# Query and key tiles on 128 partitions, the low parts of the first weights through TensorE and ScalarE, and a new table of places

## The chip, the cores and the metric

The kernel runs on one core of one Trainium2 chip. The metric is device time in microseconds (us), the median of several executions. TensorE multiplies into PSUM, VectorE, ScalarE and GpSimd do the element work, and all loads of the first stage are issued by SyncE (SP in the rows).

## What is computed

A stabilised linear attention with gates, then a dense layer with a softmax and a layer norm, then a mixture of eight experts with one expert for each token:

```
m = max(f + m, i);  C = exp(f + m_old - m) C + exp(i - m) v k^T;  n likewise with k
y = sigmoid(o) * (C q) / max(|n q|, 1)               # B=4, H=8, S=768, D=40
x = y as 3072 x 320
h = x @ w_in;  u = h * softmax(h);  z = layernorm(u) * g  @ w_out     # 320 -> 1024 -> 320
expert = argmax(norm(z) @ norm(emb)^T / tau);  out = gate * relu(z @ w1[e]) @ w2[e]
```

All weights come as 64-bit words and the result has to be exact to fp32, so that each weight is decoded on VectorE from integer words and split into a high and a low fp32r part, and each product is made of two or three fp32r matmuls.

## The kernel before

3072 tokens are cut into 24 blocks of 128 (`g` = 0 to 23; six blocks for each of the four batches). Every piece of work is a *step* with a key, an engine and a function; a step is added to a plan with `add(key, engine, ...)`, and the table `AT` gives each key a number. `Plan.order` sorts the steps by it, and the program is emitted in that order: each engine's queue is in order, so that an instruction whose input is late holds everything behind it on its engine.

The stages are these.

- **The start** (lines 321 to 570). SP issues the gates `gt`, the constants `cs` (which hold the identity), the embedding `em`, six loads of `w_in` (`rawwi`, 512 KB each), four of `w_out` (`rawwo`, 640 KB each) and the first blocks' `qk` (queries and keys, transposed) and `nat` (keys, values, output gates). There are four raw buffers, and each is given back by its decode. Up to eight loads are under way: SP waits for the load eight places ahead before it issues the next. VectorE decodes each raw tile in three instructions (`decode`, L408 to L410) and runs the scans over the gates (L352 to L366). TensorE transposes `w_out` (step `wtr`, L497), sums it (`cm`, L492) and multiplies it with the embedding (`ep`, L510, eight columns wide). 24 products of the identity with itself (`fill`, L577) stand between.
- `w_in` is split per piece j: ScalarE rounds it to fp32r (`whi`, `in_hi`, L428), and VectorE subtracts that from the decoded weight (`wlo`, `in_lo`, L434 and L436).
- **The blocks**. For each g: the scores S (L603), their mask `Pt` (VectorE, L608), the values `num` (L617), the carried state (L622), the new state `stc` (L627), the gate and the row X, its transpose `tpx` (L651), then the first dense layer `mm1` (L666 to L671; it needs all of `wlo`), softmax and norm, transposes `tpu`, the second layer `mm2` (L724 to L726) and the routing.
- **The experts**. When blocks are routed, weights `wr` and rows `xgr` of each expert are loaded, transposed (`txr`, L1093), multiplied (`m1` L1115, `m2` L1154) and scattered to the result (L1168).

Of the kernel before, what the change touches and what calls it, by code (L numbers as in the profile page):

```python
# [10 lines left out]
F32R = mybir.dt.float32r  # L11
# [52 lines left out]
    "ld_c": "138",  # L64
    "ld_e": "65",
# [3 lines left out]
    "mk": "328",  # L69
    "gmax0": "62",  # L70
    "glog0": "688",
    "gsum0": "701",
    "isub0": "682",
    "iadd0": "707",
    "iexp0": "718",
    "fexp0": "712",
    "itr0": "728",
    "icp0": "735",
    "ftr0": "726",
    "fcp0": "769",  # L80
    "gmax1": "68",
    "glog1": "88",
    "gsum1": "713",
    "isub1": "162",
    "iadd1": "736",
    "iexp1": "754",
    "fexp1": "738",
    "itr1": "801",
    "icp1": "817",
    "ftr1": "787",  # L90
    "fcp1": "805",
    "bad": "733",
    "badp": "749",
    "badc": "757",
    "f_in": "39 74 26 204 333 381",
    "dec_in": "177 215 291 374 453 590",
    "whi": "230 256 332 416 494 638",
    "wlo": "253 363 351 439 534 671",
    "emb1": "169",
    "emb2": "184",  # L100
    "emb3": "337",
    "emb4": "408",
    "emb5": "428",
    "f_out": "9 349 417 495",
    "dec_out": "118 490 546 627",
    "cm": "296 307 557 588 623 629 685 704",
    "wtr": "166 335 538 545 634 599 690 697",
    "wtc": "190 350 549 561 650 628 702 724",
    "ep": "443 462 568 613 665 675 716 739",
    "cmb": "785",  # L110
    "eg": "753",
    "esum": "763",
    "ecm": "812",
    "ecmb": "822",
    "ecen": "844",
    "eohi": "853",
    "eolo": "1039",
    "cen": "873 955 803 850",
    "ohi": "907 980 827 892",
    "olo": "957 998 856 911",  # L120
    "fill": "262 279 318 345 353 362 371 379 418 427 435 454",
    "load_q": "18 231 276 116 183 908 1071 1254 1441 1733 1953 2262 2413 2654 2893 3195 3379 3566 3814 4123 4363 4588 4773 5045",
    "load_n": "91 298 158 252 849 960 1122 1307 1501 1795 2015 2326 2502 2689 2980 3230 3442 3628 3874 4177 4413 4625 4835 5093",
    "vprep": "742 841 826 887 942 1036 1199 1385 1583 1871 2142 2403 2579 2766 3088 3315 3518 3704 4000 4253 4489 4701 4913 5170",
    "tprep": "220 433 287 380 925 1057 1204 1384 1578 1886 2092 2402 2649 2770 3057 3332 3527 3706 3951 4268 4509 4735 4912 5182",
    "smat": "117 388 816",
    "pv": "770 874",
    "smm": "761 866",
    "pmul": "264 277 412 426 976 989 1118 1132 1303 1330 1497 1510 1790 1805 2011 2025 2260 2274 2428 2441 2685 2699 2916 2930 3226 3240 3377 3391 3564 3577 3870 3883 4121 4186 4362 4421 4620 4647 4771 4785 5043 5103 5291 5304 5448 5462 5627 5641",
    "state": "773 880 1070 1253 1440 1952 2261 2412 2658 2892 3378 3565 3813 4122 4365 4772 5044 5239 5437 5580",  # L130
    "den": "791 912 1086 1270 1439 1732 1979 2287 2466 2653 2944 3194 3405 3591 3837 4135 4375 4587 4798 5056 5241 5436 5604 5882",
    "og": "823 924 1098 1282 1476 1769 1991 2299 2478 2665 2956 3206 3417 3603 3849 4147 4387 4600 4810 5068 5253 5476 5654 5894",
    "xdup": "848 959 1147 1312 1513 1794 2039 2325 2512 2707 3006 3251 3441 3635 3898 4176 4412 4624 4850 5102 5302 5500 5711 5939",
    "xtr": "857 993 1183 1333 1601 1812 2118 2408 2650 2786 3017 3274 3458 3653 3975 4256 4451 4713 4860 5123 5329 5576 5794 5953",
    "xh": "870 1004 1194 1344 1643 1830 2129 2424 2697 2803 3040 3286 3474 3664 3987 4278 4462 4725 4879 5134 5345 5592 5806 5966",
    "xl": "901 1028 1212 1358 1660 1843 2143 2455 2712 2822 3054 3303 3491 3677 3999 4298 4480 4755 4898 5159 5370 5616 5849 5985",
    "mm1": "916 956 1101 1148 1296 1340 1483 1608 1818 1855 2041 2077 2268 2304 2472 2508 2749 2792 2981 3024 3201 3238 3373 3413 3616 3714 3903 3939 4129 4174 4370 4415 4595 4631 4806 4867 5050 5087 5247 5283 5444 5481 5675 5712 5878 5917 6061 6098",
    "negmax": "1003 1187 1380 1686 1896 2119 2345 2549 2833 3065 3278 3453 3754 4010 4215 4455 4672 4945 5127 5332 5521 5753 5961 6141",
    "expo": "1032 1216 1409 1715 1924 2151 2373 2577 2862 3093 3307 3483 3783 4039 4243 4484 4700 4973 5156 5360 5550 5781 6000 6186",
    "umul": "1061 1245 1451 1744 1954 2186 2404 2606 2891 3134 3336 3512 3812 4068 4272 4513 4729 5002 5216 5389 5579 5810 6029 6215",  # L140
    "lnstat": "1091 1274 1480 1773 1983 2243 2432 2636 2920 3196 3365 3542 3841 4097 4302 4542 4759 5046 5245 5419 5608 5840 6058 6252",
    "lnvar": "1119 1317 1529 1803 2012 2273 2461 2670 2950 3224 3394 3576 3871 4145 4338 4571 4788 5074 5276 5449 5637 5876 6090 6282",
    "lnrs": "1150 1348 1561 1834 2043 2333 2492 2701 2982 3285 3426 3607 3902 4187 4369 4603 4819 5106 5306 5480 5668 5928 6134 6313",
    "utr": "1090 1138 1288 1474 1644 1592 1892 1804 1987 2032 2256 2463 2454 2581 2740 2731 2972 2963 3190 3317 3449 3608 3599 3696 3884 3893 4117 4165 4358 4406 4583 4668 4851 4843 5039 5235 5320 5432 5667 5658 5786 5837 6052 6043 6174 6220 6303 6349",
    "uh": "1105 1151 1300 1518 1657 1631 1904 1858 2000 2045 2300 2488 2500 2602 2791 2779 2989 2977 3205 3341 3462 3623 3612 3715 3904 3960 4133 4181 4377 4419 4599 4681 4868 4855 5055 5251 5333 5477 5716 5699 5816 5903 6065 6133 6211 6268 6330 6387",
    "ul": "1146 1167 1316 1533 1673 1647 1920 1874 2038 2061 2321 2504 2518 2632 2809 2795 3007 2993 3253 3361 3478 3641 3627 3731 3919 3976 4172 4199 4408 4435 4633 4696 4885 4871 5089 5318 5356 5496 5732 5715 5836 5935 6097 6166 6240 6285 6359 6407",
    "mm2": "1249 1435 1519 1556 1728 1767 1948 1996 2125 2161 2418 2545 2659 2695 2888 2927 3060 3101 3281 3465 3560 3660 3809 3848 3986 4022 4211 4263 4458 4494 4677 4767 4907 4944 5139 5336 5585 5621 5749 5801 5964 6001 6137 6184 6267 6312 6401 6438",
    "rl": "1478 1596 1839 2057 2201 2614 2735 3000 3141 3508 3700 3915 4065 4303 4535 4815 4998 5385 5664 5841 6050 6224 6353 6478",
    "rsq": "1484 1602 1845 2062 2207 2620 2741 3011 3147 3514 3727 3920 4069 4309 4540 4821 5003 5391 5670 5847 6077 6230 6358 6483",
    "ry": "1496 1615 1870 2075 2220 2633 2754 3025 3160 3536 3740 3933 4082 4322 4553 4834 5016 5404 5683 5860 6117 6242 6371 6505",  # L150
    "inter": "893",
    "att": "1007 1190 1376 1675 1900 2197 2350 2590 2829 3137 3326 3501 3750 4059 4299 4531 4720 4980 5177 5374 5517 5846",
    "rlog": "2074 3020 3932 4831 5861 6299 6487",
    "rnorm": "2086 3032 3944 4844 5872 6335 6500",
    "ridx": "2082 3028 3940 4839 5868 6307 6496",
# [1409 lines left out]
```

## Time and profile before

| what | us |
|---|---|
| median of 3 runs (563.48 to 567.12) | 563.53 |
| the profiled execution's own time | 564.77 |
| its span, first to last instruction | 562.8 |
| first `mm1` product begins | 61.18 |
| last row written | 553.51 |

The profile page gives busy shares, a strip of 40 slices, the queues, the chain that ended last and the costliest groups. In this kernel the chain that ended last has only two pieces, so that the timeline, the windows (busy time in a stretch) and the waits of TensorE tell more. Where a matmul row has twice as many instructions as products, the product is a plain fp32 one, which runs as two. The granted clock is 1.00 (2.4 GHz) or 0.50 (1.2 GHz); a window between them holds some of both.

### The profile page before, as it was taken

What the parts mean: (1) busy time and instruction counts of PE and PEld (TensorE: products, weight loads), DVE (VectorE), ACT (ScalarE), POOL (GpSimd) and SP (SyncE); (2) the same over time, 40 slices, a digit from 0 to 9 for tenths busy, and PEclk for the clock granted to TensorE, in tenths of its full rate; (3) what the DMA queues carried; (4) which work ended last, traced back from release to release, by engine and by line L of the source; (5) the groups of instructions that cost most, each with busy time, mean ns of one, the idle gap of its engine ahead of it and who ended that gap; (6) DMA issues with size and microseconds to landing.
All of it is one profiled execution on the core that took longest, in us unless ns stands there. A gap on an engine that the chain in (4) does not pass through costs nothing. (4 is left out here: it accounts for less than half of the span.)

```text
span 562.8 us, 11735 instructions
## 1 busy us (share of the span) xinstructions
PE 521.1 (93%) x4529; PEld 482.1 (86%) x4529; DVE 343.5 (61%) x756; ACT 271.2 (48%) x593; POOL 201.5 (36%) x354
## 2 busy tenths in 40 slices
PE   1869999999999999999999989789999999999992
PEld 1757889999988998899889888679999999999992
DVE  7675874677466657567766776777654363647210
ACT  1324455555655646455555764534543453637220
POOL 2001731256237326326412784671183421111112
PEclk9967799999999999999999989989999999999996
DMA  8940342324325223332330502782485353643000
GB/s 277 283 187 2 106 127 67 99 75 126 92 68 153 73 93 97 96 99 92 91 146 1 152 8 76 243 259 88 139 259 161 111 147 107 194 133 101 14 27 29
DMA packets 19897, 66.12 MB, mean 117 GB/s; under 512 B 2579, under 2 KB 5723, under 8 KB 19832
## 3 DMA queue, kind: packets, MB, share of 16 engines
q1 hardware_dynamic: 16856, 56.31, 33.0%
q0 software_dynamic: 2976, 8.96, 4.9%
q8 instruction: 38, 0.62, 0.5%
q14 instruction: 27, 0.22, 0.1%
HBM read 56.60 MB, written 8.91 MB: 116 GB/s over the span
## 5 line engine op out<-in xcount | busy, mean ns | idle before, releaser
L1136 DVE SCALAR_TENSOR_TENSOR uu<-hpu,uu 128x384 fp32r<-128x384 f32 (+2 forms) x104 | 39.8, 413 | 61.1 <-ACT uu L1131 60.9
L1131 ACT ACTIVATE uu<-hpu 128x448 fp32r<-128x448 f32 (+4 forms) x72 | 33.7, 473 | 68.4 <-PE hpu L1119 60.2
L724 PE MATMUL Y<-OH,uh 128*128 128x328 f32 x192 | 63.2, 329 | 0.0
L1168 POOL DMA_INDIRECT out_x<-you,sidx x28 | 28.8, 1027 | 93.7 <-ACT you L1161 89.2
L1154 PE MATMUL ypu<-hr,uu 128*128 128x320 f32 (+1 forms) x192 | 60.8, 317 | 0.0
L725 PE MATMUL Y<-OL,uh 128*128 128x328 f32 x192 | 60.5, 315 | 0.0
L726 PE MATMUL Y<-OH,ul 128*128 128x328 f32 x192 | 60.4, 315 | 0.0
L1156 PE MATMUL ypu<-hr,uu 128*128 128x320 f32 (+1 forms) x192 | 59.9, 312 | 0.4 <-DVE uu L1136 0.4
L1155 PE MATMUL ypu<-lr,uu 128*128 128x320 f32 (+1 forms) x192 | 59.9, 312 | 0.0
L1073 DVE TENSOR_TENSOR lr<-wr,hr 128x1024 fp32r<-128x1024 f32 (+1 forms) x32 | 43.1, 1356 | 13.2 <-ACT hr L1066 13.1
L1115 PE MATMUL hpu<-exhr,hr 128*128 128x448 f32 (+4 forms) x144 | 48.6, 337 | 2.6 <-DVE uu L1136 2.6
L716 DVE TENSOR_TENSOR ul<-tpu,uh 128x512 fp32r<-128x512 f32 x48 | 32.5, 687 | 24.5 <-ACT uh L712 24.4
L1117 PE MATMUL hpu<-exlr,hr 128*128 128x448 f32 (+4 forms) x144 | 47.3, 328 | 0.0
L1116 PE MATMUL hpu<-exhr,lr 128*128 128x448 f32 (+4 forms) x144 | 47.3, 328 | 0.0
L1066 ACT CAST hr<-wr 128x1024 fp32r<-128x1024 f32 (+1 forms) x40 | 44.7, 1138 | 3.9 <-PE ypu L1156 1.6
L680 ACT ACTIVATE e<-H,nmx 128x1024 f32<-128x1024 f32 x24 | 26.8, 1116 | 34.1 <-DVE nmx L675 34.0
L592 POOL TENSOR_TENSOR nat<-nat,wT 128x328 f32<-128x328 f32 x24 | 18.1, 757 | 68.3 <-ACT wT L377 41.2
L675 DVE TENSOR_REDUCE nmx<-H 128x1 f32<-128x1024 f32 x24 | 29.3, 1223 | 21.5 <-PE H L671 20.7
L666 PE MATMUL H<-WH,xh 128*128 128x512 f32 x96 | 40.9, 426 | 0.0
L1082 POOL DMA_INDIRECT xgr<-ys,gidx x28 | 29.4, 1050 | 28.9 <-issue 19.3
L712 ACT CAST uh<-tpu 128x512 fp32r<-128x512 f32 x48 | 27.5, 585 | 24.0 <-PE tpu L708 23.8
L667 PE MATMUL H<-WL,xh 128*128 128x512 f32 x96 | 37.9, 395 | 0.0
(239 smaller groups left out, 1382.3 us busy)
## 6 DMA issues: line engine op xcount, KB each, us to landing
wr<-in_w SPq DMA_DIRECT2D x24, 512.0 KB
nat<-in_nat SPq DMA_DIRECT2D x24, 484.0 KB
wr<-in_w SPq DMA_DIRECT2D x16, 640.0 KB
qk<-in_qkT SPq DMA_DIRECT2D x24, 416.0 KB
ys<-yr SPq DMA_DIRECT2D x5, 770.0 KB
rawwi<-in_w_in SPq DMA_DIRECT2D x6, 512.0 KB
rawwo<-in_w_out SPq DMA_DIRECT2D x4, 640.0 KB
ys<-yr SPq DMA_DIRECT2D x2, 385.0 KB
```

What stands on the lines that cost most here:

```text
L666: T.matmul(out=o, lhsT=xh[:, kk, :], rhs=WH[:, kk, f], start=(kk == 0), stop=False)
L724: T.matmul(out=yp, lhsT=uh, rhs=OH[:, k, :], start=(k == 0), stop=False)
L725: T.matmul(out=yp, lhsT=uh, rhs=OL[:, k, :], start=False, stop=False)
L726: T.matmul(out=yp, lhsT=ul, rhs=OH[:, k, :], start=False, stop=(k == 7))
L1066: A.copy(out=R.h[i], in_=R.raw[i])
L1073: eng.tensor_tensor(out=R.l[i], in0=R.raw[i], in1=R.h[i].bitcast(F32), op=ALU.subtract)
L1115: T.matmul(out=o, lhsT=R.h[k][:, fs_], rhs=xh[:, k, tk], start=(k == 0), stop=False)
L1116: T.matmul(out=o, lhsT=R.l[k][:, fs_], rhs=xh[:, k, tk], start=False, stop=False)
L1117: T.matmul(out=o, lhsT=R.h[k][:, fs_], rhs=xl[:, k, tk], start=False, stop=False)
L1154: T.matmul(out=yp, lhsT=uh, rhs=hi, start=(f == 0), stop=False)
L1155: T.matmul(out=yp, lhsT=uh, rhs=lo, start=False, stop=False)
L1156: T.matmul(out=yp, lhsT=ul, rhs=hi, start=False, stop=(f == 7))
```

## The change

1. The `qk` tile has 128 rows instead of 104 (the last 24 are zeros; `carried` reads the first 104), so that each load is 512 KB instead of 416 KB.
2. The low part of each `w_in` piece is formed on TensorE: the identity times the decoded weight (fp32), plus minus the identity times the rounded one (fp32r), both into one PSUM bank of the tag T (step `wd`). ScalarE copies the bank to where VectorE wrote before (`wlo`). ScalarE forms minus the identity once (`neg`).
3. All of the table `AT` is new, with two more keys, so that nearly every engine's order differs.

```diff
 AT = {
     "ld_g": "2",
-    "ld_c": "138",
+    "ld_c": "18",
...
+    def in_diff(j):
+        k, f = fcols(j)
+        d = wts["d", j] = bank("T", f"wd{j}")
+        T.matmul(out=d, lhsT=ident, rhs=wts["f", k][:, f], start=True, stop=False)
+        T.matmul(out=d, lhsT=negi, rhs=wts["WH"][:, k, f], start=False, stop=True)
+
+    def in_diff_cp(j):
+        k, f = fcols(j)
+        if k < 2:
+            A.copy(out=wts["WL"][:, k, f], in_=wts["d", j])
+        else:
+            A.copy(out=wts["WH"][64:, k, f], in_=wts["d", j][64:])
+
+    negi = tl("sg", [P, P], "negi", dt=F32R)
+    add("neg", "A", lambda: A.mul(negi, ident, -1.0), after=["ld_c"])
...
-        add(("wlo", j), "V", lambda j=j: in_lo(j, V), after=[("whi", j)])
+        add(("wd", j), "P", lambda j=j: in_diff(j), after=[("whi", j), "neg", "ld_c"], take="T")
+        add(("wlo", j), "A", lambda j=j: in_diff_cp(j), after=[("wd", j)], give=[(("wd", j), 0)])
...
-        s["qk"] = tl("ld", [QR, 2, NP, P], "qk" + name, "qk")
+        s["qk"] = tl("ld", [P, 2, NP, P], "qk" + name, "qk")
...
-    qkT = qk.reshape(NG, P, 2 * NP * P)[:, :QR]
+    qkT = qk.reshape(NG, P, 2 * NP * P)
```

The first rows of SP's queue, before (`rawwo` and `rawwi` are raw tiles of `w_out` and `w_in`):

```order
L321 DMA gt<-in_gates 32x1536
L397 DMA rawwo_151<-in_w_out 128x1280
L582 DMA qk_153<-in_qkT 104x1024
L397 DMA rawwi_155<-in_w_in 128x1024
L397 DMA rawwi_158<-in_w_in 128x1024
L323 DMA em<-in_emb 8x320
L397 DMA rawwi_163<-in_w_in 128x1024
L589 DMA nat_167<-in_nat 128x968
L582 DMA qk_169<-in_qkT 104x1024
L322 DMA cs<-in_cst 128x801
```

The same place of the change:

```order
L323 DMA gt<-in_gates 32x1536
L399 DMA rawwo_152<-in_w_out 128x1280
L324 DMA cs<-in_cst 128x801
L607 DMA nat_155<-in_nat 128x968
L399 DMA rawwo_158<-in_w_out 128x1280
L399 DMA rawwo_163<-in_w_out 128x1280
L325 DMA em<-in_emb 8x320
L399 DMA rawwo_170<-in_w_out 128x1280
L607 DMA nat_178<-in_nat 128x968
L399 DMA rawwi_198<-in_w_in 128x1024
L607 DMA nat_210<-in_nat 128x968
L600 DMA qk_227<-in_qkT 128x1024
```

The constants move from the tenth load to the third, all of `w_out` comes ahead of `w_in`, and the first `qk` is the twelfth load instead of the third. The last piece of `w_in` is now the last load but one of the start; before it stood ahead of the last two of `w_out`.

TensorE's queue before, from the last parts of `w_out` to the first state product:

```order
L492 MATMUL wcm<-of_359,cs 128x320
L497 MATMUL tpw_387<-cs,of_359 128x128 x2
L497 MATMUL tpw_387<-cs,of_359 64x128
L497 MATMUL tpw_391<-cs,of_359 128x128 x2
L497 MATMUL tpw_391<-cs,of_359 64x128
L492 MATMUL wcm<-of_359,cs 128x320
L510 MATMUL wep<-enT,wt_396 128x8 x3
L375 MATMUL tpf_410<-cs,fl 128x32
L375 MATMUL tpi_412<-cs,gt 128x32
L510 MATMUL wep<-enT,wt_407 128x8 x3
L384 MATMUL badp<-bad,one_123 1x1
L627 MATMUL stc_429<-nat_167 40x41 x8
```

The same place of the change (`wd` is the bank of the new products, `negi` minus the identity):

```order
L528 MATMUL wep<-enT,wt_293 128x8 x3
L528 MATMUL wep<-enT,wt_297 128x8 x3
L443 MATMUL wd_318<-wf_276,cs 128x512
L444 MATMUL wd_318<-WH,negi 128x512
L377 MATMUL tpi_325<-cs,gt 128x32
L515 MATMUL tpw_327<-cs,of_245 128x128 x2
L515 MATMUL tpw_327<-cs,of_245 64x128
L528 MATMUL wep<-enT,wt_315 128x8 x3
L515 MATMUL tpw_342<-cs,of_245 128x128 x2
L515 MATMUL tpw_342<-cs,of_245 64x128
```

The gate's transposes now stand among the products of `w_out` and not behind them, and the sums `cm` are all ahead of this place.

## Rows read from the trace of the kernel before

**Rows 1.** The page's first part: busy time, share, instructions of each engine.
```profile
PE 521.1 (93%) x4529; PEld 482.1 (86%) x4529; DVE 343.5 (61%) x756; ACT 271.2 (48%) x593; POOL 201.5 (36%) x354
```
**Rows 2.** Waits of TensorE: line, what ended them, us, times, longest.
```profile
PE tpw L497 <- DMA cs<-in_cst: 6.6, 1, 6.6
PE tpw L497 <- DVE of L410: 5.6, 1, 5.6
```
**Rows 3.** Windows: stretch, length, busy us of PE, PEld, DVE, ACT, POOL, clock, DMA, GB/s.
```profile
30.00:35.00 5.00, 0.00 (x0) 0.00 (x0) 3.86 (x6) 0.62 (x1) 0.00 (x0) 0.69 0.91 350
...
40.00:45.00 5.00, 5.00 (x17) 3.66 (x15) 4.56 (x11) 1.04 (x3) 0.00 (x0) 0.50 0.00 0
45.00:50.00 5.00, 4.48 (x29) 3.81 (x28) 1.83 (x3) 1.86 (x8) 0.00 (x0) 0.94 0.00 0
50.00:55.00 5.00, 4.88 (x73) 4.50 (x75) 2.26 (x11) 3.21 (x11) 0.99 (x2) 0.74 0.02 3
...
60.00:65.00 5.00, 5.00 (x34) 4.13 (x31) 3.97 (x9) 1.50 (x4) 3.96 (x3) 0.74 0.51 109
...
80.00:300.00 220.00, 220.00 (x2414) 198.77 (x2413) 143.74 (x327) 121.92 (x297) 89.05 (x186) 1.00 0.32 97
```
**Rows 4.** Timeline of TensorE: start, us, line, tiles, form, count.
```profile
16.68 0.87 PE L497 MATMUL tpw<-cs,of 128*128 128x128 f32 x3 [6.56 <-DMA cs<-in_cst]
...
22.20 2.40 PE L577 MATMUL H<-cs 128*128 128x128 f32 x20
...
28.78 0.83 PE L510 MATMUL wep<-enT,wt 128*128 128x8 f32 x6
...
48.08 0.82 PE L497 MATMUL tpw<-cs,of 128*128 128x128 f32 x6
...
48.73 0.70 PE L492 MATMUL wcm<-of,cs 128*128 128x320 f32 x2
...
54.79 2.08 PE L603 MATMUL S<-qk 40*128 40x128 f32 x16
...
61.18 0.80 PE L666 MATMUL H<-WH,xh 128*128 128x512 f32 x1
...
66.02 1.16 PE L603 MATMUL S<-qk 40*128 40x128 f32 x16
67.12 1.13 PE L617 MATMUL num<-nat,Pt 128*64 128x41 f32 x32
```
**Rows 5.** Timeline of SP's queue: start of the issue, us, line, load.
```profile
5.77 0.34 SPq L322 DMA_DIRECT2D cs<-in_cst  x1
8.02 0.33 SPq L589 DMA_DIRECT2D nat<-in_nat  x1
9.20 0.33 SPq L582 DMA_DIRECT2D qk<-in_qkT  x1
...
15.67 0.34 SPq L589 DMA_DIRECT2D nat<-in_nat  x1
16.61 0.33 SPq L397 DMA_DIRECT2D rawwi<-in_w_in  x1
18.15 0.33 SPq L397 DMA_DIRECT2D rawwo<-in_w_out  x1
```
**Rows 6.** Timeline and line view: decode, mask, centring, rounding, and the low parts.
```profile
25.18 0.69 DVE L409 SCALAR_TENSOR_TENSOR wf<-rawwi,wf 128x512 int32<-128x512 int32 x1
...
26.52 1.28 DVE L608 TENSOR_TENSOR Pt<-S,cs 128x512 f32<-128x512 f32 x2
...
53.78 0.96 DVE L543 SCALAR_TENSOR_TENSOR of<-of,cs,cmb 128x320 f32<-128x320 f32 x2
...
22.86 0.62 ACT L428 CAST WH<-wf 128x512 fp32r<-128x512 f32 x1 [2.98 <-DVE wf L410]
...
L434 DVE TENSOR_TENSOR WL<-wf,WH x4: 682/688/693, 19.0 to 27.7; 128x512 fp32r<-128x512 f32 x4
```
**Rows 7.** A window between the blocks and the experts, columns as rows 3.
```profile
355.00:360.00 5.00, 2.67 (x17) 2.21 (x16) 4.10 (x25) 1.47 (x2) 3.74 (x4) 1.00 0.96 339
```

More of the change, by code (lines that the diff above doesn't have):

```diff
@@ L621, in carried @@
             for j in range(2):
-                T.matmul(out=num[halves(j), 2 * p:2 * p + 2, :], lhsT=s["qk"][:, 0, p, halves(j)], rhs=c[:, p, :], start=(start and p == 0), stop=(p == NP - 1))
+                T.matmul(out=num[halves(j), 2 * p:2 * p + 2, :], lhsT=s["qk"][:QR, 0, p, halves(j)], rhs=c[:, p, :], start=(start and p == 0), stop=(p == NP - 1))
     def outer(s, stc, start, stop):
@@ L838, in moe_kernel @@
         ci = min(c, 1)
-        add(("load_q", g), "S", lambda g=g, s=s, q=q: load_q(s, qkT[g], q), war=[of("smat", g - nq), of("inter", g - nq)], size=426)
+        add(("load_q", g), "S", lambda g=g, s=s, q=q: load_q(s, qkT[g], q), war=[of("smat", g - nq), of("inter", g - nq)], size=524)
         add(("load_n", g), "S", lambda g=g, s=s, q=q: load_n(s, nat[g], q), war=[("og", g - nn), of("smm", g - nn), of("pv", g - nn)], size=496)
```

262 rows, old and new, of the table AT are left out of this document.

## The prediction

> **What bounds the kernel now.** I read the page's first part, then the waits of TensorE, the windows, and the timeline of the first 70 us. TensorE is busy for 93% of the span [rows 1], far above VectorE (61%) and ScalarE (48%), so that the time is made of three things: when TensorE's unbroken work starts, at which clock it runs, and what it waits for later. From 80 to 300 us TensorE is busy throughout at the full clock [rows 3]; nothing is to be had there. Its long waits lie in the start: 6.6 us for the constants and 5.6 us for a decode of `w_out` [rows 2]. The clock was low there too. The windows give two low stretches: of 30 to 35 us a clock of 0.69 means 3.1 us at half, then two whole windows (35 to 45) and 0.6 us, 13.7 us in all; then 2.6 + 5 + 2.6 = 10.2 us around 50 to 65 us [rows 3]. The first followed 5.6 us in which TensorE stood still. The second did not: TensorE was busy for 4.48 and 4.88 us of 5 before and at the fall, but with eight-column products, transposes and 41-column products [rows 3]. So the first `mm1` product begins only at 61.18 us [rows 4]. From there to the last row written are 492 us, with some 9.4 us of idle TensorE between 315 and 380 us (nine of thirteen windows are short; one stands in [rows 7]).
>
> The clock in the records reads 1.00 before 30 us, but the durations say otherwise: three transpose instructions took 0.87 us at 16.68 and six took 0.82 us at 48.08; identity products ran ten in 2.40 us from 22.20 on [rows 4]. So TensorE's work at 16.68 us ran at half speed, and 5.5 us later it did not.
>
> **The change, part by part.** I ask one question of all parts: when does the first `mm1` product begin? Ahead of it stand, before and after, the same blocks' products (S of three blocks, `num` of two), all of `w_out` and the gates; what follows is the same work in a different order, and I take its 492 us as they are.
>
> *Constants earlier.* The constants cost one step of SP's queue, 0.94 us (15.67 to 16.61, where SP waits for each landing in turn), and come right behind the first `w_out`, whose landing let SP go on at 5.77 [rows 5]. So TensorE can start at 6.7 instead of 16.68 us and, going by the new order, always has work: the first decode is done by then or soon after, and what the queue lacks the identity products fill.
>
> *TensorE's work up to the first `mm1`*, at full clock: 24 identity products, ten of them in 2.40 us, 5.8 us; eight sets of transposes at 0.41, 3.3; eight sums at 0.70, 5.6; eight `ep` at 0.83, 6.6; three S at 1.16, 3.5; two `num` at 1.13, 2.3 [rows 4]. The other small ones (gates' transposes, two `stc`, one carried state, `tpe`, one `tpx`) I put at 4.0, an estimate by their columns against S and `num`.
>
> *The new products* have no row. One is fp32, 512 columns: the sum's 0.70 us for 320 columns makes 1.12; the other is fp32r, 512 columns: 0.80 us at half clock, so 0.40, [rows 4] of which most overlaps its neighbour. Bounds 1.0 and 1.5 us for a pair, 6.0 and 9.0 for six; I take 1.3, 7.8 in all. They lie on TensorE's queue and count in full.
>
> The sum is 38.9 us. With 2.8 us lost to the half-speed start (5.5 us doing the work of half), `mm1` begins at 6.7 + 38.9 + 2.8 = 48.4 us, if no engine is later and the clock holds.
>
> *Who else could be last?* VectorE loses six subtractions of 0.69, 4.1 us [rows 6]. After S of block 0 (which TensorE ends at 33.9 by the same sum) its queue holds two pairs of masks (1.28 each), two decodes (1.8 each: two instructions of 0.69 and a shorter one), two pairs of centrings (0.96 each) [rows 6] and nine small ones, some 4 us: 12.1 us, where TensorE has 14.5. So the subtraction's removal is hidden by 2.4 us; left on VectorE, its share there would have eaten this. ScalarE gains six copies and one scaling, each about the 0.62 of a rounding [rows 6], 4.3 us; in the windows of [rows 3] up to 65 us it is busy for at most 3.2 of 5 us, and only the last copy is near the path, covered by a `num`, a carried state and an S (about 3 us). If that cover went, 0.6 us would be paid.
>
> *Padding.* A `qk` of 104 rows took 2.25 us of the queue (5.77 to 8.02), a `w_in` of 512 KB 1.18 and a `nat` of 484 KB 1.54 [rows 5]. A padded `qk` has no row: between 1.18 (it loads as `w_in` does) and 2.25 (its pace stays). The last `w_in` piece has ahead of it the constants 0.9, three `w_out` 4.4, four `nat` 6.2, four `qk` 4.7 to 9.0, and five other `w_in`; with itself it lands at 29.1 to 33.4 us. VectorE cannot reach it before 33.9 + 1.3 + 1.8 + 1.0 and some, about 38.9. So the padding costs nothing and gains nothing in the start; from 80 us on the DMA engines are busy for a third of the time [rows 3]. Without the 5.5 us of cover, each `qk` would be worth up to 1.1 us.
>
> *The clock.* The new order has, after the sums, five `ep` with transposes between before anything wide, as before at 45 to 52 us. So I expect one low stretch, as long as the shorter one of before: 10.2 us, losing 5.1. `mm1` then begins at 53.5, 7.7 us earlier than 61.2. Half a dozen fp32 products of 512 columns follow, denser than what stood there, which speaks against a second stretch.
> The Trainium skill (TensorE: Matmul & The Clock Gate, HAM oscillation) ties the fall of the clock to TensorE standing idle; by that alone this start, which never stands still, would keep the full clock, and the sum would be 48.4 us. The trace differs: the second fall came with TensorE busy.
>
> The profiled execution took 564.77 us, 1.2 us above the median of 563.53. A gain of 7.7 from either gives 557.1 for such a profile and **555.8** as the median.
>
> **Rivals.**
> - *No low stretch.* For it: no idle gap, wide products early. Against: the fall at 50 to 55 us with TensorE busy [rows 3]. `mm1` at 48.4, gain 12.8: 550.7.
> - *Two low stretches, as before.* For it: the region from the first `ep` to S of block 2 is long and thin, and before had two. Against: the new wide products. `mm1` at 58.6, gain 2.6: 560.9.
> - *Slower: the clock falls at the first `ep`, near 22 us, and stays low until `mm1` itself.* In that stretch TensorE's work is 26 us; at half speed it takes 52 and `mm1` begins at 74: 13 us slower, 576. It decides from 25.6 us of low clock on (half of that is the 12.8 gained). For it: before, the second stretch ended only after S, `num` and `mm1`. Against: the first one ended among transposes, sums and `ep`.
> - *The gain is given back between blocks and experts.* The order there is new: 24 `m1` products now stand ahead of the last `mm2` instead of 16, and nine weight loads instead of six ahead of the last stores. TensorE stands idle for 9.4 us there before; more loads early may take some 4 us off, `m1` work used up early may add as much [rows 7]. Price 4 us either way: 552 or 560.
>
> **How the numbers follow.** Chances: one low stretch 0.42, none 0.20, two 0.25, given back (or gained) at the experts 0.07, low all along 0.06. The predicted time is that of the first. The bounds of the new products (1.8 us down, 1.2 up), the length of the stretch (13.7 instead of 10.2 costs 1.8 more) and the experts' 4 us spread each case by about 3. From the case of no stretch, less 1.7, to that of two, plus 1.1, is 549 to 562; what lies outside is the slow case and the tails. About 1%, 5.6 us, is what a measurement of this kernel can tell from no change. Faster by more means below 557.9: most of the first case, all of the second, little of the third, 0.62. Slower by more: 0.07. Within: 0.31.
>
> **What would show it.** The first `fill` near 6.7 us; the `wd` rows at 1.0 to 1.5 us a pair; the last `w_in` decoded without a wait for its load; no wait of TensorE of several us before `mm1`; the first `mm1` product near 53.5, with half clock in about two windows of 5 us before it. The distance from it to the last row written stays near 492 us. I am wrong if `mm1` begins on time and that distance grows, if VectorE or ScalarE ends TensorE's waits ahead of `mm1`, or if the clock is low for more or less than one such stretch.

## The result and the profile after

The changed kernel takes 547.75 us (median of 4, 545.20 to 547.92), the kernel before beside it 563.50: ratio 0.9699, 95% interval 0.9652 to 0.9746. It is faster by more than was predicted (555.8 us), and lies 1.25 us below the low end of the range. The profiled execution took 547.71 us with a span of 545.8.

Executions of one program differ here by some 8 us, and with them the mean granted clock: beside e13 to e16 the kernel before took 561.06 us at a clock of 0.967 and 569.20 at 0.951. The ratios below leave disturbed executions out (three of e12's six and one of e13's among them), so that they aren't quite the quotients of the medians.

The page's first part for the changed kernel, as [rows 1]:

```profile
PE 522.0 (96%) x4547; PEld 480.5 (88%) x4547; DVE 336.4 (62%) x750; ACT 275.7 (51%) x600; POOL 200.5 (37%) x354
```

TensorE is as busy as before, in a span that is 17.0 us shorter. Its waits (line, what ended them, us, times, longest), as [rows 2]:

```profile
PE H L595 <- DMA cs<-in_cst: 6.7, 1, 6.7
PE txr L1111 <- DVE ovt L1277: 2.6, 1, 2.6
PE txr L1111 <- DMA xgr<-ys,gidx: 2.2, 2, 1.7
PE hpu L1133 <- DVE uu L1154: 0.5, 1, 0.5
...
PE wep L528 <- ACT enT L492: 0.3, 1, 0.3
PE ip L835 <- DVE ohv L829: 0.2, 1, 0.2
```

Of the start only the constants at 6.7 us and 0.3 us for the embedding are left; the wait for a decode of `w_out` is gone. So is the longest wait of before, which the prediction does not name, for the first `qk`:

```profile
PE S L603 <- DMA qk<-in_qkT: 8.0, 1, 8.0
```

Ahead of its first `mm1` TensorE waited for 20.7 us before (8.0, 6.6 and 5.6, and 0.5 for ScalarE) and waits for 6.9 now. The clock (windows with the columns of [rows 3]: busy us of PE, PEld, DVE, ACT, POOL, clock, DMA share, GB/s):

```profile
20.00:25.00 5.00, 4.74 (x34) 4.23 (x33) 4.03 (x6) 3.05 (x12) 0.00 (x0) 0.98 1.03 409
25.00:30.00 5.00, 5.00 (x21) 3.35 (x20) 0.00 (x0) 1.70 (x5) 0.74 (x1) 0.50 0.64 252
30.00:35.00 5.00, 5.00 (x43) 4.78 (x44) 4.00 (x7) 3.86 (x11) 0.85 (x1) 0.50 0.00 0
35.00:40.00 5.00, 5.00 (x21) 3.63 (x20) 3.63 (x7) 0.82 (x3) 0.69 (x1) 0.50 0.33 105
40.00:45.00 5.00, 5.00 (x45) 2.93 (x45) 4.01 (x10) 3.23 (x6) 0.80 (x2) 0.81 0.02 5
```

It is low in one stretch, 0.2 + 15 + 1.9 = 17.1 us, from 24.8 to 41.9, and TensorE never stands still in it. TensorE's timeline, as [rows 4]:

```profile
6.65 2.07 PE L595 MATMUL H<-cs 128*128 128x128 f32 x8 [6.65 <-DMA cs<-in_cst]
...
13.68 1.24 PE L510 MATMUL wcm<-of,cs 128*128 128x320 f32 x4
...
20.59 1.78 PE L528 MATMUL wep<-enT,wt 128*128 128x8 f32 x12 [0.26 <-ACT enT L492]
...
36.43 1.54 PE L528 MATMUL wep<-enT,wt 128*128 128x8 f32 x6
37.91 2.07 PE L443 MATMUL wd<-wf,cs 128*128 128x512 f32 x2
...
40.20 1.87 PE L443 MATMUL wd<-wf,cs 128*128 128x512 f32 x2
41.12 1.19 PE L444 MATMUL wd<-WH,negi 128*128 128x512 f32 x1
...
43.72 1.13 PE L443 MATMUL wd<-wf,cs 128*128 128x512 f32 x2
...
44.92 1.02 PE L443 MATMUL wd<-wf,cs 128*128 128x512 f32 x2
...
52.00 0.50 PE L684 MATMUL H<-WH,xh 128*128 128x512 f32 x1
```

The first `mm1` product begins at 52.00 instead of 61.18 us, so that 9.2 of the 17.0 us lie ahead of it: 13.8 us of waits are gone, six pairs at 1.2 us (below) are new, and some 2.6 are left over, which fits the shorter low clock (17.1 us instead of 23.9). The last row is written at 536.47 us (GpSimd's timeline), 484.5 us behind it instead of 492.3:

```profile
536.47 0.91 POOL L1186 DMA_INDIRECT out_x<-you,sidx  x1 [0.78 <-DVEq L1487]
```

### The profile page after: what moved, and what is told of

The parts are those of the page before. It is cut to its first block, busy times and chain, and to the rows that moved or that the text cites. A ratio compares the mean times of both kernels' runs of the same rounds, so it can differ in the third digit from the quotient of the medians.

```text
span 545.8 us, 11754 instructions
## 1 busy us (share of the span) xinstructions
PE 522.0 (96%) x4547; PEld 480.5 (88%) x4547; DVE 336.4 (62%) x750; ACT 275.7 (51%) x600; POOL 200.5 (37%) x354
## 5 line engine op out<-in xcount | busy, mean ns | idle before, releaser
L1172 PE MATMUL ypu<-hr,uu 128*128 128x320 f32 (+1 forms) x192 | 59.6, 311 | 0.0
L1174 PE MATMUL ypu<-hr,uu 128*128 128x320 f32 (+1 forms) x192 | 59.3, 309 | 0.0
L693 DVE TENSOR_REDUCE nmx<-H 128x1 f32<-128x1024 f32 x24 | 29.4, 1225 | 33.2 <-PE H L689 31.0
L684 PE MATMUL H<-WH,xh 128*128 128x512 f32 x96 | 39.8, 415 | 0.4 <-DVE u L703 0.4
L1100 POOL DMA_INDIRECT xgr<-ys,gidx x28 | 31.6, 1129 | 20.9 <-DVE ovt L1260 7.1
L685 PE MATMUL H<-WL,xh 128*128 128x512 f32 x96 | 37.6, 392 | 0.0
L703 DVE SCALAR_TENSOR_TENSOR u<-e,H 128x1024 f32<-128x1024 f32 x24 | 29.2, 1218 | 12.6 <-ACT e L698 12.4
```

Source lines behind the costliest of these rows:

```text
L1172: T.matmul(out=yp, lhsT=uh, rhs=hi, start=(f == 0), stop=False)
L1174: T.matmul(out=yp, lhsT=ul, rhs=hi, start=False, stop=(f == 7))
```

## The experiments

The last two columns are of each run's profiled execution: where the first `mm1` begins, and the us from there to the start of the last row.

| run | median | before beside it | ratio (95%) | `mm1` | to the end |
|---|---|---|---|---|---|
| before, first profile | 563.53 | | | 61.18 | 492.3 |
| e9 before again, one execution | 566.64 | | | 65.93 | 489.3 |
| the change | 547.75 | 563.50 | 0.9699 (0.9652 to 0.9746) | 52.00 | 484.5 |
| e5 the change again | 547.51 | 565.47 | 0.9713 (0.9667 to 0.9759) | 51.77 | 483.9 |
| e1 new start alone | 550.45 | 565.82 | 0.9726 (0.9681 to 0.9771) | 52.73 | 488.5 |
| e2 new rest alone | 562.58 | 565.82 | 0.9953 (0.9926 to 0.9981) | 63.73 | 486.6 |
| e3 104 rows | 549.64 | 565.82 | 0.9723 (0.9690 to 0.9756) | 52.44 | 485.8 |
| e4 low parts on VectorE | 551.86 | 565.82 | 0.9774 (0.9733 to 0.9816) | 53.43 | 486.0 |
| e14 order alone | 551.77 | 564.79 | 0.9747 (0.9693 to 0.9802) | 53.96 | 487.0 |
| e15 padding alone | 561.65 | 564.79 | 0.9945 (0.9914 to 0.9976) | 59.66 | 490.4 |
| e16 low parts on TensorE alone | 559.06 | 564.79 | 0.9887 (0.9832 to 0.9942) | 57.46 | 490.0 |
| e10 constants alone | 563.93 | 565.21 | 1.0008 (0.9977 to 1.0039) | 61.51 | 490.3 |
| e6 two identity products | 547.46 | 565.47 | 0.9702 (0.9651 to 0.9754) | 52.32 | 485.7 |
| e7 identity products later | 550.64 | 565.47 | 0.9748 (0.9702 to 0.9795) | 55.15 | 486.5 |
| e8 more of them | 551.06 | 565.47 | 0.9749 (0.9701 to 0.9798) | 57.50 | 485.1 |
| e11 one low part on VectorE | 546.79 | 565.21 | 0.9667 (0.9636 to 0.9697) | 50.40 | 486.9 |
| e12 four on VectorE | 551.45 | 565.21 | 0.9690 (0.9627 to 0.9753) | 53.41 | 486.5 |
| e13 wide products early | 549.41 | 564.79 | 0.9695 (0.9645 to 0.9745) | 53.86 | 488.0 |
| e17 wide products spread | 553.35 | 566.26 | 0.9762 (0.9716 to 0.9807) | 57.11 | 486.6 |
| e18 spread, one on VectorE | 552.06 | 566.26 | 0.9753 (0.9724 to 0.9783) | 55.14 | 485.8 |

### How much is the start, how much the rest: e1, e2, e9, e5

e1 is the changed kernel with all steps from number 837 on (the first `mm1`) sorted as before; e2 is the kernel before up to its first `mm1` (916) and the new order behind it. Both tables are numbered anew, for instance in e1 and in e2:

```diff
-    "open_r": "5649",
+    "open_r": "956",
...
-    "open_r": "5936",
+    "open_r": "924",
```

> The changed kernel up to the first `mm1` product; every step that the new table puts behind it stands in the order of the table before. Theory (the 17.0 us between the two profiled executions are two separate gains): the start keeps its 9.2 us and the low clock at 61 to 63 us of before is gone too (0.7 us), and so is the 0.6 us that TensorE stood idle right behind the first `mm1`; the boundary between blocks and experts goes back to before, with 3.5 us more idle TensorE and one more low stretch of 3.4 us (1.7 us): first `mm1` at 52, from there to the last row about 491 us, median 553 to 554. Rival (the later 7.8 us follow from the earlier start, not from the order there): 547 to 548 again.

> The converse: the kernel before (104-row tiles, low parts on VectorE) up to its first `mm1` product, and every later step in the order of the new table. Theory: first `mm1` near 61, the boundary as in the changed kernel (some 6 us of idle TensorE instead of 9.4, one short low stretch instead of two): 557 to 559. Rival (the later gain needs the earlier start): 562 to 564.

By the first two profiles the rest is worth 7.8 us. e2 gives 2.7 us for it (0.47%, interval 0.2 to 0.7%; its 562.58 lies in the rival's range, but the kernel before took 565.82 beside it), and e1, without it, is within the error of the whole change. So both expectations, built on the first profiles, put too much of the gain into the rest. It is there, though: in the fourteen profiles with the new order of the rest the last column is 483.9 to 488.0 us (mean 486.1), in the six with the old one 488.5 to 492.3 (mean 490.1). The waits of TensorE in e1 show its place:

```profile
PE txr L1111 <- DMA xgr<-ys,gidx: 3.2, 3, 2.0
PE hpu L1133 <- DVE uu L1154: 2.7, 5, 1.3
PE ip L835 <- POOL ohv L829: 1.4, 1, 1.4
```

With the old order the `m1` products of the experts wait 2.7 us for their inputs from VectorE and the routing's `ip` 1.4; in the changed kernel and in e2 0.5 and 0.2.

> The kernel before itself, profiled again. In its first profile the clock was low for 10.2 us around 50 to 65 us, and for twice 3.4 us between blocks and experts; in the run with the same start and the new order behind it the first of these was 17.2 us long and `mm1` came at 63.73 instead of 61.18. Theory (the low clock differs between executions of one and the same order, and the first profile had a short one in the start): a stretch of another length, `mm1` between 61 and 65, and another sum of low time between 315 and 380 us. Rival (it belongs to the order): 10.2 us and 61.2 again, twice 3.4 us.

The kernel before, profiled again, was low from 30 to 68 us without a break (windows):

```profile
30.00:35.00 5.00, 0.00 (x0) 0.00 (x0) 3.87 (x7) 0.62 (x1) 0.00 (x0) 0.52 0.77 262
...
50.00:55.00 5.00, 5.00 (x23) 4.40 (x21) 0.00 (x0) 2.42 (x9) 0.73 (x1) 0.50 0.00 0
...
65.00:70.00 5.00, 5.00 (x30) 4.08 (x27) 3.96 (x9) 1.50 (x4) 3.71 (x3) 0.72 0.52 125
```

That is 4.8 + 30 + 2.8 = 37.6 us at half clock, where the first profile had 23.9 in two stretches some 7 us apart [rows 3]. The queue is the same, and `mm1` begins 4.75 us later, 0.9 beyond what was expected. The theory holds otherwise: the low time belongs to the execution as much as to the order. The first profile of before was one with an early `mm1` (61.2; the others with its start order have 63.7 and 65.9) and a long rest (492.3; the others in the old order 488.5 to 490.4).

> The changed kernel itself, in the same hour and on the same chip as the other runs, since the kernel before took 565.8 us beside the first four runs and 563.5 beside the first measurement. Theory: its distance to the kernel before stays 15 to 17 us (549 to 551 beside 565.8), and its low stretch between the `ep` products and the first `mm1` is again some 17 us long. Rival (the length of the stretch differs between executions of the same order, as 10.2 us in the profile of before and 17.2 us in the run that has the same start): 10 to 20 us, and `mm1` between 49 and 54.

On the chip of the experiments the change keeps its distance (2.9% against 3.0%; by the medians 18.0 us, where 15 to 17 were expected), and its low stretch is again 17.1 us long (a clock of 0.94 from 20 us on, three windows at 0.50, one at 0.85). The rival, another length, doesn't show here.

### The parts alone and undone: e3, e15, e4, e16, e14, e10

```diff
-        s["qk"] = tl("ld", [P, 2, NP, P], "qk" + name, "qk")
+        s["qk"] = tl("ld", [QR, 2, NP, P], "qk" + name, "qk")
...
-    qkT = qk.reshape(NG, P, 2 * NP * P)
+    qkT = qk.reshape(NG, P, 2 * NP * P)[:, :QR]
```

> The changed kernel with `qk` tiles of 104 rows. Theory of the prediction (padding is hidden): the first loads take longer, each 104-row load about 1 us more than a padded one, so that the last `w_in` lands near 34 instead of 30.5 us; VectorE decodes it at 41 us, so that the time stays within 0.5% of the changed kernel, 546 to 549.5. Rival (the quick loads carry the early start; in the kernel before, all loads together ran at 290 to 318 GB/s against 409 to 420 now): `mm1` 3 to 7 us later, 550 to 555.

Windows of e3:

```profile
10.00:15.00 5.00, 5.00 (x38) 4.53 (x37) 4.83 (x8) 1.16 (x4) 1.45 (x2) 1.00 1.02 408
15.00:20.00 5.00, 4.74 (x32) 3.73 (x30) 4.77 (x11) 1.18 (x5) 0.00 (x0) 1.00 1.03 314
```

Up to 15 us the loads run at 408 GB/s; when the 104-row loads come all loads together run at 314, with the DMA engines as busy (1.03), where they keep 409 with the padded ones. e15 and the kernel before differ in the same way, 399 to 413 against 290 to 318 between 5 and 25 us. Still `mm1` moves by only 0.4 to 0.7 us, and the intervals of e3 and the change overlap: in the changed order the padding is hidden, or worth about the 2 us between the medians; the runs don't tell which. e15 is the reverse edit in the kernel before.

> The kernel before with padded `qk` tiles and nothing else. Its loads run at 290 to 318 GB/s, and TensorE waits for the decode of a late `w_out` from 30 to 35.6 us. Theory of the prediction (padding gains nothing): within 0.3% of the kernel before. Rival (the loads quicken to about 410 GB/s as in the changed kernel, and the last `w_out` lands 5 to 7 us earlier): the wait at 30 to 35 us shrinks by 3 to 5 us, ratio 0.990 to 0.996.

There it gives 3.1 us (0.55%, interval 0.2 to 0.9%). The waits of TensorE in e15:

```profile
PE tpw L497 <- DMA cs<-in_cst: 5.4, 1, 5.4
...
PE tpw L497 <- DVE of L410: 2.9, 1, 2.9
```

The wait for the late decode of `w_out` falls from 5.6 to 2.9 us [rows 2], a little less than the rival had it, and the loads and the ratio are as it had them: the rival was right for that order.

For e4 the low parts go back to VectorE:

```diff
-        add(("wd", j), "P", lambda j=j: in_diff(j), after=[("whi", j), "neg", "ld_c"], take="T")
-        add(("wlo", j), "A", lambda j=j: in_diff_cp(j), after=[("wd", j)], give=[(("wd", j), 0)])
+        add(("wlo", j), "V", lambda j=j: in_lo(j, V), after=[("whi", j)])
```

> The changed kernel with the low parts of `w_in` left on VectorE, at the same numbers of the table: TensorE loses six pairs of products (7.2 us at full clock), ScalarE six copies, VectorE gains six subtractions of 0.69 us. Theory of the prediction (TensorE sets the start, VectorE has some room): `mm1` comes 2 to 5 us earlier, 543 to 546. Rival one (VectorE sets it, since it has only some 5 us of gaps between 30 and 52 us and the subtractions stand behind roundings): no gain or slower, 547 to 551. Rival two (the wide products are what ends the low clock at 42 us): without them the clock stays low longer, `mm1` later by up to 4 us, 548 to 552.

Slower than the change, by 4.4 us between the medians. The wait and the windows of e4:

```profile
PE tpx L664 <- DVE X L655: 5.6, 1, 5.6
```
```profile
40.00:45.00 5.00, 1.59 (x24) 1.15 (x22) 4.93 (x5) 1.19 (x2) 3.95 (x4) 0.50 0.00 0
45.00:50.00 5.00, 2.47 (x33) 2.17 (x35) 4.79 (x12) 1.36 (x5) 0.00 (x0) 0.50 0.31 99
```

Both rivals: VectorE is busy for 4.9 of 5 us and TensorE waits 5.6 us for it, and the clock stays low for 34.2 us, into the first `mm1`, instead of 17.1. This profile can't tell whether the clock stayed low for want of wide products or because TensorE stood waiting; e12 below tells more. e16 forms the low parts on TensorE in the kernel before.

```diff
-        add(("wlo", j), "V", lambda j=j: in_lo(j, V), after=[("whi", j)])
+        add(("wd", j), "P", lambda j=j: in_diff(j), after=[("whi", j), "neg", "ld_c"], take="T")
+        add(("wlo", j), "A", lambda j=j: in_diff_cp(j), after=[("wd", j)], give=[(("wd", j), 0)])
...
+    "neg": "139",
+    "wd": "252 362 350 438 533 670",
```

> The kernel before with the low parts of `w_in` through TensorE and ScalarE (each pair of products and each copy just ahead of where the subtraction stood in the table) and nothing else. Theory (in that order the decode of the last `w_out` sets the start, and it waits for its load): TensorE does some of the pairs in its idle time, and `mm1` stays within 2 us, ratio 0.994 to 1.003. Rival (VectorE freed of 4.1 us decodes the last `w_out` earlier, and the wide products shorten the low clock): `mm1` 3 to 6 us earlier, ratio 0.988 to 0.994.

It gives 6.4 us (1.1%, interval 0.6 to 1.7%), as the rival had it. Windows of e16:

```profile
30.00:35.00 5.00, 5.00 (x30) 3.83 (x30) 3.61 (x6) 1.42 (x3) 0.00 (x0) 1.00 0.90 320
...
45.00:50.00 5.00, 4.88 (x72) 4.41 (x72) 1.11 (x9) 3.60 (x13) 0.73 (x1) 0.82 0.01 3
```

The five us from 30 on, in which TensorE stood still before [rows 3], are full, at full clock, and the low time is 10.3 us in all; the wait for the decode of `w_out`, 5.6 us before, isn't among its waits.

The mean granted clock of each execution says the same without a profile. With the low parts on VectorE it is 0.949 to 0.964 in e4's six executions, on TensorE 0.971 to 0.981 in e5's six; in the old order 0.951 to 0.969 in the 17 of the kernel before beside e16, and 0.975 to 0.990 in e16's four. So the low parts on TensorE come with less time at half clock in both orders.

e14 takes the edits of e3 and e4 together, so that only the new order is left.

> The new table alone: the changed kernel with `qk` tiles of 104 rows and all low parts on VectorE, at the numbers of the table. Theory (the parts of the change add up: padding some 2 us, the low parts on TensorE some 4, the order the rest of 18): 553 to 555, ratio 0.977 to 0.982. Rival one (with slow loads the subtractions on VectorE collide, so that the parts need each other): 556 to 562. Rival two (each undone part is covered by the other): 551 to 552.5.

The order alone gives 14.3 us (2.5%, interval 2.0 to 3.1%). It comes without a higher clock: 0.956 to 0.964 in e14's four executions, within the 0.951 to 0.969 of the kernel before beside it. The parts don't add up: 14.3 + 3.1 + 6.4 is 23.8, the whole 15.8 to 18.0 by the medians, 16.2 to 17.0 by the ratios. Each covers a piece of what another would save: padding (e15) and low parts (e16) shorten a wait for `w_out` that the new order doesn't have.

```diff
-    "ld_c": "138",
+    "ld_c": "18",
```

> The kernel before with one number changed: the constants are the third load instead of the tenth. Theory (the order of `w_out` decides, the constants alone do little): TensorE starts near 7 us instead of 16.7 but still waits for the decodes of the last two parts of `w_out`, which land behind all of `w_in`: `mm1` within 1.5 us of the kernel before, time within 0.5% of it. Rival (TensorE's start is what counted): `mm1` 5 to 9 us earlier, ratio 0.985 to 0.99.

In the kernel before, the constants alone do nothing. The waits of TensorE in e10:

```profile
PE S L603 <- DMA qk<-in_qkT: 14.6, 2, 9.2
PE tpw L497 <- DVE of L410: 4.3, 1, 4.3
```

Its transposes do begin earlier, at 11.23 instead of 16.68 us, but its first product, an S, begins later (9.22 instead of 8.05), and the waits for `qk` grow from 8.0 to 14.6 us; with the late decode they come to 18.9 us where the kernel before had 20.2 with its constants, and `mm1` stands where it was. So a new place for the constants needs new places for other loads too. Whether those of `qk` or of `w_out` count for more was not tested.

### What holds the clock: e6, e7, e8, e11, e12, e13, e17, e18

```diff
-NFILL = 12
+NFILL = 1
```

> The changed kernel with one `fill` step of two identity products instead of twelve steps of 24: 22 products, 5.3 us at full clock, are gone ahead of the sums. Theory (the identity products stand where TensorE would wait for the decodes of `w_out` and for the embedding's transposes, which come at 20 us whatever TensorE does): TensorE stands idle for about 5 us between 8 and 20 us, the first `ep` stays near 20.6, `mm1` within 1 us of the changed kernel if the clock does the same. Rival one (the idle time brings the clock down earlier): low from 15 to 20 us on, `mm1` 2 to 5 us later, total 552 to 555 on this chip. Rival two (they delay the sums and what follows): `mm1` up to 5 us earlier, 545 to 547.

Windows of e6:

```profile
15.00:20.00 5.00, 3.94 (x22) 2.83 (x21) 4.77 (x11) 1.74 (x7) 0.00 (x0) 0.93 1.03 411
20.00:25.00 5.00, 5.00 (x19) 4.11 (x18) 4.25 (x6) 1.78 (x6) 0.00 (x0) 0.50 1.02 409
```

TensorE stands still for 1.6 us between 8 and 20, not for 5, and the first `ep` begins at 17.99 instead of 20.59 us, so that the identity products did cost time there. But the clock falls at 19.3 instead of 24.8 us and the low time is 23.9 us instead of 17.1. The two cancel: `mm1` is 0.3 to 0.5 us later and the time the same, 547.46 against 547.51. The theory's `mm1` came out, by another way than it said. e7 has 16 of the 24 identity products between the `ep` products, e8 has 16 more there:

```diff
-    "fill": "125 142 207 215 224 232 259 274 293 302 311 319",
+    "fill": "125 142 207 215 372 397 407 430 460 485 503 515",
```

> The changed kernel with the same 24 identity products, of which 16 stand between the `ep` products (20 to 37 us) instead of among the sums. Theory (the clock falls because that stretch holds only products that are eight columns wide, transposes and 41-column products): the stretch at half clock becomes shorter than 17 us or falls into pieces, which gives back up to 6 us; against it stand 3.9 us of products that now lie on the busy part, and as much idle time ahead of it. Together `mm1` between 48 and 53, total 545 to 551 on this chip. Rival (the low clock does not depend on these products): `mm1` 4 to 6 us later, total 554 to 557.

> The changed kernel with all 24 identity products where they are and 16 more of them between the `ep` products: 3.9 us more work at full clock. Theory as in the run before: if the clock holds, 8.5 us are given back for 3.9, `mm1` near 47 to 49, total 545 to 547 on this chip. Rival: the clock falls all the same, `mm1` at 56 to 59, total 554 to 558.

In e7 the clock comes back inside the window from 30 us (0.77) and is gone again in the next (0.57); e8 shows the same some 2 us later:

```profile
30.00:35.00 5.00, 5.00 (x47) 4.33 (x45) 3.13 (x6) 2.38 (x9) 0.00 (x0) 0.77 0.00 0
```

It came back at 32.3 and 34.7 us, among transposes, identity products and a state product, with the last pair of wide products some 6 us back. So wide products are not the only thing at which a low stretch ends. The low time is 20.5 us in two pieces in each, and `mm1` is 3 and 5.5 us later. The stretch fell into pieces, as the theory had it, without the gain; the times, 550.64 and 551.06 us, lie between those of theory and rival for e8 and within the theory's for e7.

e11 takes piece 0 alone from TensorE, e12 pieces 0 to 3, with the decodes moved into VectorE's idle time:

```diff
+        if j in (0, 1, 2, 3):
+            add(("wlo", j), "V", lambda j=j: in_lo(j, V), after=[("whi", j)])
+            continue
...
-    "dec_in": "344 447 505 542 626 683",
+    "dec_in": "344 447 450 455 470 553",
```

> The changed kernel with the low part of the first `w_in` piece on VectorE and the other five on TensorE. VectorE stands idle from 24.1 to 30.1 us there (it waits for a transpose of `w_out` ahead of the next centring), so that the subtraction of 0.69 us has room, and TensorE loses the pair that took 1.9 us at half clock. Theory (TensorE sets the start): `mm1` 1 to 2 us earlier, time 545.5 to 547. Rival (the clock takes it back, or VectorE is as near to the end as TensorE): 547 to 549.

> The changed kernel with the low parts of four pieces on VectorE, and its queue put in another order for it: the decodes of the pieces 2 to 4 and the four subtractions stand in the 6 us in which VectorE waits between 24 and 30 us, and the centring that waits stands behind them. Only the two pieces of 64 rows stay on TensorE. Theory (in the run with all low parts on VectorE at the old numbers it was VectorE's order that cost 4.4 us, and TensorE's work is the bound): TensorE loses four pairs, 4.8 us at full clock and 7.5 us where they stood; `mm1` at 45 to 49, time 541 to 545. Rival (the wide products are what ended the low clock at 42 us): the clock stays low until `mm1` and longer, `mm1` at 49 to 53, time 546 to 551.

e11's `mm1` is 1.4 us earlier, as expected, but its time isn't told from the change's by the intervals. e12 tells more. Behind the constants TensorE never waits longer than 0.7 us, VectorE has room, and still `mm1` comes at 53.41; its windows and two of its pairs:

```profile
40.00:45.00 5.00, 5.00 (x30) 3.26 (x30) 1.52 (x5) 1.12 (x3) 0.78 (x2) 0.50 0.34 102
...
55.00:60.00 5.00, 5.00 (x19) 3.80 (x17) 0.98 (x3) 0.72 (x1) 2.29 (x2) 0.65 0.22 82
```
```profile
36.35 2.07 PE L443 MATMUL wd<-wf,cs 128*128 128x512 f32 x2
...
38.78 1.94 PE L638 MATMUL num<-nat,Pt 128*64 128x41 f32 x32
40.65 2.08 PE L443 MATMUL wd<-wf,cs 128*128 128x512 f32 x2
```

With 41-column products between the two pairs the clock stays low for 34.1 us, to 58.5, where wide `mm1` products stand. One of its six executions took 543.47 us, at a mean clock of 0.976; the others 551.0 to 553.5 at 0.955 to 0.963, so that the ratio flatters e12 and the median, 551.45, doesn't. The rival holds: TensorE does less work and waits for nothing long, and the low clock takes the gain back.

e13 moves three pairs side by side to 28 us, and no work is changed:

```diff
-    "wd": "415 597 619 674 696 751",
+    "wd": "4150 4490 4520 4570 5950 6500",
```

(the other numbers are ten times the old, but for the decodes, roundings and copies that go with them). 

> The changed kernel with its start put in another order: VectorE decodes the pieces 1 to 4 of `w_in` one behind the other (the centring that waits 6 us for a transpose stands later), ScalarE rounds them at once, and the pairs of wide products of pieces 1, 2 and 3 stand side by side behind the fifth `ep`, about 28 us, instead of at 38, 40 and 44 us. No work is added or left out. Theory (several wide products side by side end the low clock, narrow ones do not): the stretch at half clock ends near 34 to 36 instead of 42 us, `mm1` at 47 to 49, time 543 to 545. Rival (the length of the stretch does not depend on where they stand): `mm1` within 1 us of the changed kernel's 51.8 to 52, 547 to 549.

Windows of e13, whose profile caught the slowest of its six executions (553.44 us):

```profile
30.00:35.00 5.00, 5.00 (x11) 2.38 (x9) 1.63 (x3) 1.91 (x4) 0.00 (x0) 0.56 0.00 0
35.00:40.00 5.00, 5.00 (x62) 4.54 (x60) 0.93 (x2) 3.68 (x12) 0.00 (x0) 1.00 0.00 0
...
45.00:50.00 5.00, 4.00 (x58) 3.15 (x59) 4.44 (x8) 2.89 (x8) 3.63 (x4) 0.81 0.33 101
50.00:55.00 5.00, 5.00 (x51) 4.41 (x48) 3.34 (x10) 1.26 (x3) 2.23 (x2) 0.50 0.37 109
```

The first half of the theory holds: the stretch ends at 34.4 us, at the end of the three pairs (28.31 to 34.7), 7.5 us earlier. The second, `mm1` at 47 to 49 and 543 to 545 us, doesn't: a new stretch of 10.2 us begins at 48 us, behind the last pair, in a window in which TensorE is also busy for only 4.00 of 5 us. Whether the narrow products or the waits brought it on isn't shown. e17 and e18 spread the pairs to avoid it, e18 with piece 0 on VectorE:

```diff
-    "wd": "4150 4490 4520 4570 5950 6500",
+    "wd": "4150 4490 4520 5300 5950 7510",
```

> As the run with the wide products early, but only the pairs of pieces 1 and 2 stand side by side at 28 to 33 us; piece 3 stands ahead of the first S (near 35), piece 4 behind the last `ep` (near 39), piece 5 behind the second state product (near 46), so that no narrow run longer than some 5 us is left. No work is added or left out. Theory (wide products end the low clock, and a long run of narrow ones brings it back, as from 46.4 us on in that run): the first stretch ends near 35 us and none follows before `mm1`, which begins at 47 to 49: 542 to 545. Rival: a second stretch all the same, `mm1` at 51 to 54, 547 to 550.

> The same with the low part of the first piece on VectorE, which has decoded two pieces by then: TensorE loses the pair that stands at 24 us. Theory (TensorE's work is the bound, and this pair stands where the clock falls): `mm1` 1 to 2 us earlier than in the run with six pairs, 541 to 544. Rival (the pair is one of those that hold the clock up): the low stretch begins earlier or lasts longer, and the time is that of the run with six pairs or 1 to 3 us more.

Windows of e17:

```profile
30.00:35.00 5.00, 4.46 (x26) 2.13 (x24) 2.22 (x4) 1.89 (x4) 0.00 (x0) 0.68 0.00 2
35.00:40.00 5.00, 5.00 (x23) 3.62 (x23) 0.00 (x0) 2.39 (x9) 0.00 (x0) 0.66 0.00 0
40.00:45.00 5.00, 5.00 (x25) 3.88 (x25) 2.11 (x5) 1.29 (x3) 0.00 (x0) 0.50 0.28 87
```

The low clock ends at 33.2 us, with two pairs side by side, is back at 36.6 among eight-column products, and stays through the single pairs at 37.9 and 44.1 us to 53.7, the end of the third at 51.8. e18 has the same low time in its profile, 23.9 us, and without the first pair its `mm1` comes 2.0 us earlier, as expected. Both miss their times, 542 to 545 and 541 to 544. Spread came out slower than side by side, 553.35 against 549.41, but the two intervals overlap, and none of these orders is measurably faster than the change. What starts a stretch, and why its length differs between executions, stays open.

## Why the prediction was wrong

**Baseline and distance: the step that failed.** The prediction said of the stage from the first `mm1` to the end: "what follows is the same work in a different order, and I take its 492 us as they are". It came out at 484.5. The new order of the rest was put at nothing without a reason, and the two terms of before, `mm1` at 61.18 us and the 492 us, were taken from one profile as if they belonged to the order. The profiled execution is 9.4 us below the 557.1 forecast for it: 7.9 of them are here, 1.5 at `mm1`. One part is real: the new order of the rest, 2.7 us by e2 (1.1 to 4.2 by its interval), 4.1 between the means of the profiles. Only the rival between blocks and experts held it, and with a chance of 0.07 for both its signs. Its price of 4 us was near, its reason (early loads) not what showed: `m1` and `ip` no longer wait for VectorE and GpSimd. The other part was the profile of before itself. It had two stretches of 3.4 us at half clock between blocks and experts (windows of the kernel before), where the change and e5 have one, and e9, in the same order as before, has one too (e2, in the new order, has 6.8 us in one, so that this too belongs to the execution):

```profile
330.00:340.00 10.00, 8.62 (x55) 8.39 (x54) 6.37 (x20) 5.71 (x13) 7.19 (x14) 0.83 0.00 0
...
370.00:380.00 10.00, 7.99 (x50) 7.37 (x48) 7.06 (x19) 2.71 (x7) 7.13 (x10) 0.83 0.78 261
```

And its `mm1` at 61.18 was early for that order (63.73 in e2, 65.93 in e9). So the start is worth more than the 9.2 us of the first two profiles, and more than the 7.7 us forecast: e1 gains 15.4 us by the medians. In the means of the profiles the start gives 11.4 us (63.6 against 52.2, three profiles each), the rest 4.1, together 15.5. How much of the gap each stage holds is known only as far as `mm1` scatters, by 4.75 us in the old order.

**Start of TensorE.** At 6.65 us, expected 6.7; right. But before it did not start at 16.68: its first S began at 8.05, behind the 8.0 us for `qk`, a wait that the prediction left out and the longest of the start. e10 shows that the early constants need other changes of the order to be of use.

**The sum of the start.** 38.9 us was too much. By the rows of after, the sums take 0.62 instead of 0.70 each (four rows, two sums, 1.24), the transposes some 0.33, the pairs 1.2 (43.72 to 44.92; the bounds were 1.0 to 1.5), the small ones 3.1, and the other terms are nearly what was set: about 36.

**The clock.** One stretch, as forecast, but 17.1 us instead of 10.2. 6.65 + 36 + 2.5 for the half speed in the beginning + 0.3 of waiting makes 45.5, so that by difference some 6.5 us are left for the stretch, where 5.1 had been set. Here too a length from one execution was taken for a property of the order. An `ep` of three products took 1.54 us there against 0.89 at full clock, less than twice as long, which fits a cost below half the length. The two errors, 2.9 too much work and 1.4 too little loss, go against each other, and the 6.5 is what is left over; that `mm1` came within 1.5 us is in part luck.

The Trainium skill (TensorE: Matmul & The Clock Gate, HAM oscillation) ties low clocks to idle TensorE. The trace differs, as weighed in the prediction: the stretch of after lies in windows of 5.00 busy us of 5. It ended with two pairs of wide products side by side, as in e5, e13 (three pairs) and the first of e17; in e7 and e8, and in the kernel before, which has no such pairs ahead of `mm1`, a stretch ended without them.

**VectorE and ScalarE.** Right that they are not last in the changed kernel: TensorE waits for neither ahead of `mm1` but for 0.3 us. "Left on VectorE" it would have cost, and e4 gives the size: TensorE then waits 5.6 us for VectorE.

**Padding.** Costed at nothing; in the new order that is within the error (e3). But the price was taken per `qk`, when all loads together run slower while the 104-row ones are under way, and in the kernel before it is worth 3.1 us (e15).

**Range.** It let the start and the stretch vary and held the profile of before for fixed. Its `mm1` alone scatters by 4.75 us between two profiles.

## What to carry to other kernels

Profile the kernel before twice before its stages are taken as terms: here one profile put `mm1` 4.75 us earlier than the next, and shared the gain wrongly between two stages. Where TensorE is the bound and the clock falls with it busy, look at which products stand side by side: work moved to TensorE as wide products can pay for itself by the clock (e4 and e16), though where in the queue they do so best was not found here. Compare the mean granted clock of all executions, not only of the profiled one. Undo each part alone and try each alone; parts that remove the same wait don't add up.

## What had not been expected

- While 104-row loads are under way, all loads together run at 314 GB/s instead of 409, with the DMA engines as busy (1.03). The Trainium skill (DMA: Bandwidth & Descriptors, Why a DMA increments its semaphore by 16 and not by 1) says that a transfer is spread over the largest number of engines up to 16 that divides the slowest dimension of both sides, by which 104 rows would go to 13 engines and 128 to 16, eight rows each. No run here shows the engines one by one, and why the rate falls stays open.
- 24 identity products that nobody needs cost nothing and gain nothing against two (e6): in the two profiles the clock holds 5.5 us longer with them, and they take 5.3 us more.
